# Turning the global heads' attention weights by DMA instead of on TensorE, in a window-attention and FFN kernel

## The chip, the cores and the metric

The kernel runs on one NeuronCore of one Trainium2 chip. The metric is the device time of one execution in microseconds (us); lower is better. Engine names are those of the profile: PE (TensorE matmul), PEld (TensorE weight load), DVE (VectorE), ACT (ScalarE), POOL (GpSimd), SP (SyncE, which here issues nearly all DMAs).

## The reference, cut to what matters

```python
# B, H, SL, SG, D = 8, 8, 512, 32, 64
k_all = np.concatenate([k_g, k_l], axis=2)           # 544 keys
s_g   = scale * np.matmul(q_g, k_all.transpose(0, 1, 3, 2))
out_g = np.matmul(sm(s_g), v_all)                    # 32 global queries see all 544 keys
s_ll  = np.where(np.abs(i - j) <= 32, scale * q_l @ k_l.T, -1e9)
a_l   = sm(np.concatenate([scale * q_l @ k_g.T, s_ll], axis=-1))
out_l = a_l @ np.concatenate([v_g, v_l], axis=2)     # 512 local queries, window of 32
x     = concat([out_g, out_l]) as [4608, 512]
h     = x @ w_in                                     # 512 -> 2048
g     = s * relu(h) ** 2 + b
out   = g @ w_out                                    # 2048 -> 512
```

In words: in each of 8 batches and 8 heads, 32 global queries attend to 544 keys and 512 local queries attend to their window and the 32 global keys. All 4608 rows then go through a feed-forward network (FFN) with a squared ReLU.

## The kernel before, in words

The program is one loop over 146 steps j. Step j computes the scores and the softmax of local head j (128 of them: batch, half of the sequence, head), and the FFN's first product for chunk m = j - 10 (`ffn_in`, 24 matmuls, L479) and its second product for chunk m - 1 (`ffn_out`, 12 matmuls, L512). There are 136 chunks of 2 x 128 hidden columns; 8 chunks make one tile of 256 rows. From step 18 on the order of PE, ACT and DVE is the order in which the code emits instructions. SP and POOL are placed by the scheduler.

One step, as it touches the change:

- PE: scores of head j (L352) with the global heads' product (L364) in between; every fourth step the product of weights and values of four local heads (`pv`, L319); `ffn_in` (L479); `ffn_out` of the chunk before (L512).
- DVE: masked scores with their minimum (L207), the sum into the global scores (L373), the sum and its reciprocal (L217, L218), the division (L223), four copies that part the f32 weights into two planes of 16-bit halves (L385, tile `two`), then for the FFN `r` (L486) and the low part of `g` (L494). `ffn_out` needs that low part with its third weight load.
- ACT: rounds keys and queries of the next head (L191, L193), one copy for the global scores (L372), the two exponentials (L214), joins the halves of the head before, once the DMA has turned them (L395, tile `turned`), then for the FFN the ReLU (L485) and the high part of `g` (L493).
- SP: loads, and one DMA transpose of `two` into `turned` per local head (L387).

So the local heads' weights are turned by DMA: part on DVE, turn by DMA, join on ACT one step later. Only the first 16 steps turn theirs on PE.

The global heads come in groups of four, `g` = 0 and 1 of each batch. Their scores are gathered in a tile `sg` of 128 rows (4 heads x 32 queries) by 544 keys. Their steps hang on s0 = 16 b + 12 for group 0 and 16 b + 16 for group 1: softmax (`g_softmax`) in step s0, the values' load in s0 + 2 (`g_load`), the turn in s0 + 3 (`g_transposes`), the product with the values in s0 + 5 (`g_pv`). The turn is five PE transposes of 128 x 128 (L419), four before `ffn_out`'s first half and one before its second, each followed by a copy from PSUM to the tile `pg` on ACT (L420). In ACT's order these copies stand behind the high part of `g` (L493), ahead of the next head's L191.

For batch 1, which the rows below show, group 0 has its softmax in step 28 and its turn in step 31, group 1 in steps 32 and 35. Step 35's `ffn_in` is chunk 25, and its `ffn_out` is chunk 24.

Of the kernel before, what the change touches and what calls it, by code (L numbers as in the profile page):

```python
# [10 lines left out]
F32 = mybir.dt.float32  # L11
# [4 lines left out]
I16 = mybir.dt.int16  # L16
# [5 lines left out]
P = 128  # L22
# [16 lines left out]
SGW = SL + SG  # L39
# [13 lines left out]
JOINED = [("pg", 1280), ("vsg", 1280)]  # L53
X_ACT = lambda i: i >= 4
G_AT = (12, 16)
G_TR = 3
G_LD = 2
G_PV = 5
GL_POOL = lambda m: False
# [8 lines left out]
def window_attention_then_ffn(ctx: ExitStack, tc: tile.TileContext, qd, qp, qg, kw, vw, vg, w_in, w_out, sv, bv, out):  # L68
    nc = tc.nc
# [3 lines left out]
    sb = ctx.enter_context(tc.tile_pool(name="sb", bufs=2))  # L73
    ps = ctx.enter_context(tc.tile_pool(name="ps", bufs=1, space=bass.MemoryType.PSUM))
# [3 lines left out]
    ident = const.tile([P, P], F32, name="ident")  # L78
# [18 lines left out]
    for first, parts in ((True, ((32, 192, 0),)), (False, ((0, 160, 0), (192, 224, 32)))):  # L97
# [3 lines left out]
        for c0, c1, skip in parts:  # L101
            for sign, base in ((1, c0 - skip), (-1, 64 - c0 + skip)):
                nc.gpsimd.affine_select(
                    out=mask[:, c0:c1], in_=mask[:, c0:c1], pattern=[[sign, c1 - c0]], compare_op=ALU.is_ge,
# [64 lines left out]
    st_ = {}  # L169
# [85 lines left out]
    def v_load(i):  # L255
        b, hf, h = slot(2 * i)
        rv = sb.tile([P, 2, 4 * D], F32, tag="rv", name=f"rvp{i}", bufs=2)
        nc.sync.dma_start(rv, vw[b, hf, h:h + 2].rearrange("h p f -> p h f"))
        st_["rvp", i] = rv
# [70 lines left out]
    def qg_load(b):  # L330
        rqg = sb.tile([P, 264], F32, tag="xr", name=f"rqg{b}", bufs=1)[:, 0:H * SG]
        nc.sync.dma_start(rqg, qg[b])
        st_["rqg", b] = rqg

    def qg_split(b):
        rqg = st_["rqg", b].rearrange("p (h q) -> p h q", h=H)
        qgs = sb.tile([P, H, 2, SG], F32R, tag="qgs", name=f"qgs{b}", bufs=1)
        nc.scalar.copy(out=qgs[:, :, 0, :], in_=rqg)
        nc.gpsimd.tensor_sub(out=qgs[:, :, 1, :], in0=rqg, in1=f32(qgs[:, :, 0, :]))
        st_["qgs", b] = qgs  # L340
# [34 lines left out]
    def late_scores(j):  # L375
        if ("late", j) in st_:
            p_g = ps.tile([P, 512], F32, tag="g", name=f"ps_g{j}")
            g_product(j, st_.pop(("late", j)), p_g)
            g_sum(j, p_g)
# [11 lines left out]
    def join(j):  # L391
        if j % 2 == 0:
            st_["ptp", j // 2] = sb.tile([P, 2, 4, P], F32, tag="pt", name=f"ptp{j // 2}")
        pt = st_["ptp", j // 2][:, j % 2]
        nc.scalar.copy(out=pt.bitcast(I16).rearrange("p c (q h) -> p c h q", h=2), in_=st_.pop(("turned", j)))  # L395
# [4 lines left out]
    def g_softmax(b, g):  # L400
        v = st_["sg", b, g]
        gm = sb.tile([P, 1], F32, tag="gm", name=f"gm{b}_{g}")
        gs = sb.tile([P, 1], F32, tag="gs", name=f"gs{b}_{g}")
        nc.vector.reduce_max(out=gm, in_=v, axis=mybir.AxisListType.X)
        nc.vector.tensor_scalar_mul(gm, gm, -scale)
        nc.scalar.activation(out=v, in_=v, func=AF.Exp, bias=gm, scale=scale, accum_out=gs)
        nc.vector.tensor_scalar_add(gs, gs, 1e-9)
        nc.vector.reciprocal(gs, gs)
        nc.vector.tensor_scalar_mul(v, v, gs)

    def g_transposes(b, g):
        sg = st_["sg", b, g]
        pg = sb.tile([P, 1280], F32, tag="pg", name=f"pg{b}_{g}", bufs=1)[:, 0:5 * P].rearrange("p (c r) -> p c r", c=5)
        st_["pg", b, g] = pg
        for c0, c1, tag in ((0, 4, "t"), (4, 5, "o")):
            p_t = ps.tile([P, 4, P], F32, tag=tag, name=f"ps_tg{b}_{g}_{c0}")
            for c in range(c0, c1):
                s0 = min(c * P, SGW - P)
                nc.tensor.transpose(out=p_t[:, c - c0, :], in_=sg[:, s0:s0 + P], identity=ident)  # L419
            nc.scalar.copy(out=pg[:, c0:c1], in_=p_t[:, 0:c1 - c0])  # L420
            yield

    def g_load(b, g):
        rv = st_["rvg", b, g] = sb.tile([P, 4, 5, D], F32, tag="vsg", name=f"rvg{b}_{g}", bufs=1)
        nc.sync.dma_start(rv.rearrange("p h c d -> p (h c d)"), vg[b, g])

    def g_pv(b, g):
        pg, rv = st_.pop(("pg", b, g)), st_.pop(("rvg", b, g))
        p_g = ps.tile([P, 512], F32, tag="t", name=f"ps_og{b}_{g}")
        for c in range(5):  # L430
            for n in range(4):
                m = slice(SG * n, SG * n + SG)
                nc.tensor.matmul(p_g[m, 0:D], lhsT=pg[:, c, m], rhs=rv[:, n, c], start=(c == 0), stop=(c == 4))  # L433
        og = sb.tile([P, P + 40], F32, tag="og", name=f"og{b}_{g}", bufs=1)[:, 0:D]
        nc.scalar.copy(out=og, in_=p_g[:, 0:D])
        rows = xg_d[b * SG:(b + 1) * SG, 4 * g * D:(4 * g + 4) * D]
        nc.sync.dma_start(rows.rearrange("q (h d) -> h q d", h=4), og)
# [60 lines left out]

    oacc = {}

    def ffn_out(m, turn):
        t, pr = m // 8, m % 8
        g = gs_.pop(m)
        if pr == 0:
            oacc[t] = [ps.tile([P, DM], F32, tag=f"acc{i}", name=f"acc{t}_{i}") for i in range(2)]
        for i in range(2):
            next(turn, None)
            n = 0
            for k in range(2):
                f = 2 * pr + k  # L510
                for a, e in ((0, 0), (0, 1), (1, 0)):
                    nc.tensor.matmul(  # L512
                        oacc[t][i], lhsT=g[:, a, k, i * P:(i + 1) * P], rhs=wo[f][:, e, :],
                        start=(pr == 0 and n == 0), stop=(pr == 7 and n == 5),
                    )
                    n += 1
        if pr == 7:
            for i in range(2):
                o = sb.tile([P, DM], F32, tag="r", name=f"o{t}_{i}", bufs=2)
                nc.scalar.copy(out=o, in_=oacc[t][i])  # L520
                if t < 16:
                    b, hf = t // 2, t % 2
                    r0 = b * (SL + SG) + SG + hf * HALF + i * P
                    nc.sync.dma_start(out[r0:r0 + P, :], o)
                else:
                    rows = out.rearrange("(b r) d -> b r d", r=SL + SG)[4 * i:4 * i + 4, 0:SG, :]
                    nc.sync.dma_start(rows, o)
# [3 lines left out]

    ENGINES = {getattr(mybir.EngineType, e) for e in ("PE", "Activation", "DVE")}
    NM = NT * 8
    early, gpv, turns = defaultdict(list), defaultdict(list), {}
    for b in range(B):
        for g in range(2):
            s0 = 16 * b + G_AT[g]
            early[s0].append(lambda b=b, g=g: g_softmax(b, g))
            turns[s0 + G_TR] = g_transposes(b, g)
            early[s0 + G_LD].append(lambda b=b, g=g: g_load(b, g))  # L540
            gpv[s0 + G_PV].append(lambda b=b, g=g: g_pv(b, g))

# [20 lines left out]
    for j in range(NM + LAG + 2):  # L563
        if j == ORDERED:
            fixed.enter_context(tc.manual_schedule(engines=ENGINES))
        sp(j + 1)
        if j + 4 < NF:
            ld(j + 4)
        if j + 2 >= NF:
            ld(j + 2)  # L570
        if NF <= j < NS and j % 4 == 2:
            for i in (j // 2 - 1, j // 2):
                v_load(i)
        for _ in range(CHUNKS_AT[j] if j < len(CHUNKS_AT) else 0):
            weight_chunk(chunk)
            chunk += 1
        if j < NS:
            b1 = j // 16 + 1
            if j % 16 == 14 and b1 < B:
                qg_load(b1)  # L580
            sc(j)
            if j % 16 == 15 and NF <= j + 1 < NS:
                qg_split(b1)
        tr(j - 1)
        pvs(j - 2)
        if NF <= j - 5 < NS and j % 4 == 1:
            pv((j - 5) // 2, 2)
        for fn in gpv.pop(j, []):
            fn()
        if NF <= j - 1 < NS:  # L590
            join(j - 1)
        if j == 0:
            vl32(0)
        vl32(j + 2)
        m = j - LAG
        for fn in early.pop(j, []):
            fn()
        if m == -1:
            x_split(0)
        then = []  # L600
        if 0 <= m < NM:
            t = m // 8 + 1
            if m % 8 == 7 and t < 16:
                then.append(lambda: x_split(t))
            ffn_in(m, then)
            late_scores(j)
            if m % 8 == 7 and t == 16:
                xg_split(16)
        else:
            for fn in then:  # L610
                fn()
        if 0 <= m - 1 < NM:
            ffn_out(m - 1, turns.pop(j, iter(())))
        else:
            list(turns.pop(j, ()))
    fixed.close()
    assert chunk == 16 and not gpv and not early

# [74 lines left out]
```

## Time and profile before

| | us |
|---|---|
| median of 3 runs (980.45 to 981.97) | 981.84 |
| the profiled execution | 982.35 |
| its span | 980.5 |
| PE busy | 948.3 (97%) |
| PE weight load busy | 846.3 (86%) |
| ACT busy | 714.6 (73%) |
| DVE busy | 651.0 (66%) |

The profiled execution lies 0.5 us above the median, and 1.9 us of it lie outside the span. Matmuls are pipelined and their ends are modelled, so a busy PE is not a PE at its peak. The rows below come from several views: groups of instructions by line, waits by pair, the chain of waits that ended last, and the timeline of single engines in order of time, merged where equal instructions follow each other.

### The profile page before, as it was taken

The page shows a single profiled execution, that of the slowest core. Times are in us where ns is not written, and L with a number is a line of the kernel's source. Part 1 is how long each engine was busy: PE and PEld are TensorE (multiplying, and loading weights), DVE is VectorE, ACT ScalarE, POOL GpSimd, SP SyncE. Part 2 cuts the span into 40 slices and gives each one's busy share as a digit, 9 for nine tenths or more (in the row PEclk, how much of TensorE's full clock was granted, in tenths as well). Part 3 has the DMA queues.
Part 4 walks back from the last instruction along what each step waited for, and adds up shares of the span by engine and source line. Part 5 has one row for each costly group of instructions (what it writes and reads, how often), then busy time and mean ns, then how long its engine had stood idle before and what let it go on. Part 6 is the DMA issues. An engine that isn't in the chain of part 4 may idle for free.

```text
span 980.5 us, 20198 instructions
## 1 busy us (share of the span) xinstructions
PE 948.3 (97%) x7380; PEld 846.3 (86%) x7380; DVE 651.0 (66%) x1996; ACT 714.6 (73%) x1510; POOL 217.4 (22%) x245
## 2 busy tenths in 40 slices
PE   6779999999999999999999999999999999999996
PEld 2457889999999999999999999999999999998995
DVE  5998766676767776677677766777667776742321
ACT  5986687777878787788788787788778787753221
POOL 1010322322323233232223232232323232300000
PEclk7669999999999999999999999999999999999999
DMA  8944335445544555535654464454543564220000
GB/s 308 341 163 147 99 98 129 106 109 137 133 99 114 130 135 111 108 98 133 132 116 99 129 153 90 117 124 109 135 115 90 143 133 101 71 62 35 11 12 22
DMA packets 177899, 115.09 MB, mean 117 GB/s; under 512 B 126088, under 2 KB 167048, under 8 KB 177800
## 3 DMA queue, kind: packets, MB, share of 16 engines
q1 hardware_dynamic: 177512, 112.76, 44.5%
q8 instruction: 58, 0.95, 0.4%
q10 hardware_dynamic: 288, 1.05, 0.3%
q14 instruction: 41, 0.34, 0.1%
HBM read 74.97 MB, written 9.44 MB: 86 GB/s over the span
## 4 chain that ended last, share of the span: by engine, by line
PE 91%; DVE 3%; DMA 3%; ACT 1%; SPq 0%; issue 0%; POOL 0%; POOLq 0%; ACTq 0%
PE ps_h L479 39%; PE acc L512 38%; PE ps_op L319 5%; PE ps_s L352 5%; PE ps_g L364 1%; PE ps_og L433 1%; DMA wst<-in_w_in 1%; PE ps_tg L419 1%; DMA b_t<-in_bv 1%; DVE we L161 1%; DMA wst<-in_w_out 1%; DVE wst L160 1%; DMA rkp<-in_kw 1%; DVE w L165 0%; DVE we L157 0%
## 5 line engine op out<-in xcount | busy, mean ns | idle before, releaser
L479 PE MATMUL ps_h<-xs,w 128*128 128x256 f32 x3264 | 412.7, 281 | 1.5 <-DVE nm L207 1.5
L512 PE MATMUL acc<-w,g 128*128 128x512 f32 x1632 | 403.6, 395 | 0.0
L479 PEld LDWEIGHTS ps_h<-xs,w 128*128 128x128 f32 x3264 | 395.0, 189 | 7.8 <-DVE nm L207 1.8
L512 PEld LDWEIGHTS acc<-w,g 128*128 128x128 f32 x1632 | 296.0, 188 | 58.4 <-DVE g L494 0.3
L192 POOL TENSOR_TENSOR kq<-rk,kq 64x416 fp32r<-64x416 f32 x112 | 125.4, 1120 | 628.5 <-ACT kq L191 600.5
L493 ACT ACTIVATE g<-r,b_t 128x512 fp32r<-128x512 f32 x136 | 98.5, 724 | 113.0 <-DVE r L486 113.0
L494 DVE SCALAR_TENSOR_TENSOR g<-r,b_t,g 128x512 fp32r<-128x512 f32 x136 | 103.0, 757 | 103.2 <-ACT g L493 103.2
L395 ACT COPY ptp<-turned 128x1024 int16<-128x1024 int16 x112 | 152.2, 1359 | 7.0 <-DMA turned<-two 7.0
L486 DVE SCALAR_TENSOR_TENSOR r<-ps_h,s_t,r 128x512 f32<-128x512 f32 x136 | 101.8, 748 | 68.6 <-ACT r L485 68.4
L485 ACT ACTIVATE r<-ps_h 128x512 f32<-128x512 f32 x136 | 81.4, 599 | 59.8 <-PE ps_h L479 54.0
L214 ACT ACTIVATE sm<-sm,nm 128x224 f32<-128x224 f32 (+1 forms) x256 | 117.8, 461 | 4.3 <-DVE nm L207 3.1
L385 DVE COPY two<-sm 128x256 int16<-128x256 int16 x448 | 100.1, 287 | 1.0 <-DMA turned<-two 1.0
L194 POOL TENSOR_TENSOR kq<-rq,kq 128x256 fp32r<-128x256 f32 x112 | 84.5, 755 | 8.8
L207 DVE CUSTOM_DVE_ANT_0 sm<-ps_s,mask 128x192 f32<-128x192 f32 (+1 forms) x224 | 74.3, 369 | 9.7 <-PE ps_s L352 9.7
L352 PE MATMUL ps_s<-kq 128*128 128x192 f32 (+1 forms) x448 | 78.0, 265 | 0.0
L352 PEld LDWEIGHTS ps_s<-kq 128*128 128x128 f32 x448 | 71.9, 189 | 6.9
L373 DVE TENSOR_TENSOR sg<-ps_g,tg 32x256 f32<-32x256 f32 (+1 forms) x112 | 48.3, 431 | 30.4 <-ACT tg L372 26.8
L223 DVE TENSOR_SCALAR sm<-sm,ss 128x192 f32<-128x192 f32 (+1 forms) x224 | 64.9, 332 | 3.9
L217 DVE TENSOR_SCALAR ss<-ss 128x2 f32<-128x2 f32 (+1 forms) x120 | 36.4, 303 | 45.6 <-ACT sm L214 45.1
L319 PE MATMUL ps_op<-ptp,rvp 128*64 128x128 f32 (+2 forms) x1024 | 61.4, 266 | 2.5 <-ACT ptp L310 2.3
L319 PEld LDWEIGHTS ps_op<-ptp,rvp 128*64 128x64 f32 x1024 | 52.7, 143 | 10.5 <-ACT ptp L310 4.2
L191 ACT CAST kq<-rk 64x416 fp32r<-64x416 f32 x112 | 59.8, 534 | 2.0 <-PE ps_s L352 0.7
(63 smaller groups left out, 644.7 us busy)
## 6 DMA issues: line engine op xcount, KB each, us to landing
rvp<-in_vw SPq DMA_DIRECT2D x64, 256.0 KB, 2.9
rq<-in_qd SPq DMA_DIRECT2D x112, 128.0 KB, 2.3
rk<-in_kw SPq DMA_DIRECT2D x56, 208.0 KB, 2.5
rvg<-in_vg SPq DMA_DIRECT2D x16, 640.0 KB, 5.7
out<-o SPq DMA_DIRECT2D x34, 256.0 KB, 2.0
wst<-in_w_in SPq DMA_DIRECT2D x15, 512.0 KB, 4.0
wst<-in_w_out SPq DMA_DIRECT2D x15, 512.0 KB, 6.9
turned<-two SPq DMA_TRANSPOSE x112, 3.1
```

The costliest lines, as they stand in the source:

```text
L192: (nc.gpsimd if K_POOL(j) else nc.vector).tensor_sub(out=ks[p1:p1 + 64], in0=rk[p0:p0 + 64], in1=f32(ks[p0:p0 + 64]))
L194: nc.gpsimd.tensor_sub(out=qs[:, 1, :], in0=rq, in1=f32(qs[:, 0, :]))
L214: nc.scalar.activation(out=p, in_=p, func=AF.Exp, bias=nm[:, n:n + 1], scale=-1.0, accum_out=ss[:, n:n + 1],)
L319: nc.tensor.matmul(p_o[64 * k:64 * k + 64, u, blk, q0:q0 + w], lhsT=rv[:, k, v:v + D], rhs=pt[:, k, o] if i < NF // 2 else pt[:, k, 2 * bl ...
L352: nc.tensor.matmul(p_s[:, cols], lhsT=qs[:, a, blk * P:(blk + 1) * P], rhs=ks[:, cols], start=(a == 0), stop=(a == 1),)
L385: nc.vector.tensor_copy(out=two[:, 2 * blk + c], in_=sm[:, :, c0:c0 + P])
L395: nc.scalar.copy(out=pt.bitcast(I16).rearrange("p c (q h) -> p c h q", h=2), in_=st_.pop(("turned", j)))
L479: nc.tensor.matmul(p_h[:, k], lhsT=wi[f][:, a, c, :], rhs=xs[:, e, c, :], start=(n == 0), stop=(n == 11),)
L486: nc.vector.scalar_tensor_tensor(out=r, in0=p_h, scalar=s_t, in1=r, op0=ALU.mult, op1=ALU.mult)
L493: nc.scalar.activation(out=g[:, 0], in_=r, func=AF.Identity, bias=b_t)
L494: nc.vector.scalar_tensor_tensor(out=g[:, 1], in0=r, scalar=b_t, in1=f32(g[:, 0]), op0=ALU.add, op1=ALU.subtract,)
L512: nc.tensor.matmul(oacc[t][i], lhsT=g[:, a, k, i * P:(i + 1) * P], rhs=wo[f][:, e, :], start=(pr == 0 and n == 0), stop=(pr == 7 and n == 5),)
```

## The change

The five PE transposes and the two ACT copies of a group go. In step s0 + 2 DVE parts `sg` into two planes of 16-bit halves (five copies into a new tile `gtwo`) and SP issues one DMA transpose of its ten blocks of 128 x 128. In step s0 + 3 ACT joins the halves into f32 with one copy of 1280 16-bit elements a row. Both results lie in the two halves of the buffer `pg`, which keeps its size.

```diff
-G_TR = 3
+G_TR = 2
...
-    def g_transposes(b, g):
-        sg = st_["sg", b, g]
-        pg = sb.tile([P, 1280], F32, tag="pg", ...)[:, 0:5 * P].rearrange("p (c r) -> p c r", c=5)
-        for c0, c1, tag in ((0, 4, "t"), (4, 5, "o")):
-            p_t = ps.tile([P, 4, P], F32, tag=tag, ...)
-            for c in range(c0, c1):
-                s0 = min(c * P, SGW - P)
-                nc.tensor.transpose(out=p_t[:, c - c0, :], in_=sg[:, s0:s0 + P], identity=ident)
-            nc.scalar.copy(out=pg[:, c0:c1], in_=p_t[:, 0:c1 - c0])
-            yield
+    def g_turn(b, g):
+        sg = st_["sg", b, g].bitcast(I16).rearrange("p (k h) -> p h k", h=2)
+        both = sb.tile([P, 4 * 5 * P], I16, tag="pg", ...)
+        turned, pg = both[:, 0:10 * P], both[:, 10 * P:20 * P]
+        two = sb.tile([P, 5, 2, P], I16, tag="gtwo", ..., bufs=1)
+        for c in range(5):
+            s0 = min(c * P, SGW - P)
+            nc.vector.tensor_copy(out=two[:, c], in_=sg[:, :, s0:s0 + P])
+        turned = turned.rearrange("p (c h q) -> p c h q", c=5, h=2)
+        nc.sync.dma_start_transpose(turned..., two...)
+
+    def g_join(b, g):
+        turned, pg = st_.pop(("turned_g", b, g))
+        nc.scalar.copy(out=pg.rearrange("p (c q h) -> p c h q", c=5, h=2), in_=turned)
...
-            turns[s0 + G_TR] = g_transposes(b, g)
+            early[s0 + G_TR].append(lambda b=b, g=g: g_turn(b, g))
+            early[s0 + G_TR + 1].append(lambda b=b, g=g: g_join(b, g))
```

DVE, step 34 (batch 1, group 1; a name's number is the step or chunk). Before:

```order
L223 TENSOR_SCALAR sm34_2781<-sm34_2781,ss34_2780 128x224
L385 COPY two34_2793<-sm34_2781 128x256 x4
L486 SCALAR_TENSOR_TENSOR r24_2828<-ps_h24_2803,s_t_71,r24_2828 128x512
L494 SCALAR_TENSOR_TENSOR g24_2831<-r24_2828,b_t_72,g24_2831 128x512
L207 ISA sm35_2868,nm35_2866<-ps_s35_2859,mask1_104 128x192
```

DVE, step 34, in the changed kernel:

```order
L223 TENSOR_SCALAR sm34_2778<-sm34_2778,ss34_2777 128x224
L385 COPY two34_2790<-sm34_2778 128x256 x4
L418 COPY gtwo1_1_2799<-sg20_1466 128x256 x5
L493 SCALAR_TENSOR_TENSOR r24_2833<-ps_h24_2808,s_t_71,r24_2833 128x512
L501 SCALAR_TENSOR_TENSOR g24_2836<-r24_2833,b_t_72,g24_2836 128x512
L207 ISA sm35_2873,nm35_2871<-ps_s35_2864,mask1_104 128x192
```

The five copies stand between the local head's copies and the FFN's `r`.

ACT, step 35 and the start of step 36. Before:

```order
L395 COPY ptp17_2887<-turned34_2798 128x4x2x128
L485 ACTIVATE r25_2914<-ps_h25_2889 128x512
L493 ACTIVATE g25_2917<-r25_2914,b_t_72 128x512
L420 COPY pg1_1_2922<-ps_tg1_1_0_2923 128x512
L420 COPY pg1_1_2922<-ps_tg1_1_4_2935 128x128
L191 CAST kq37_2944<-rk36_2764 64x416
```

ACT at the same place in the changed kernel:

```order
L395 COPY ptp17_2892<-turned34_2795 128x4x2x128
L427 COPY pg1_1_2798<-pg1_1_2798 128x5x2x128
L492 ACTIVATE r25_2920<-ps_h25_2895 128x512
L500 ACTIVATE g25_2923<-r25_2920,b_t_72 128x512
L191 CAST kq37_2940<-rk36_2761 64x416
```

The work on `pg` moves from behind `g` of the FFN to ahead of its ReLU, and is one copy in place of two.

## Rows read from the trace of the kernel before

**Rows 1.** The page: busy time by engine, then the chain's shares by line.

```profile
PE 948.3 (97%) x7380; PEld 846.3 (86%) x7380; DVE 651.0 (66%) x1996; ACT 714.6 (73%) x1510; POOL 217.4 (22%) x245
...
PE ps_h L479 39%; PE acc L512 38%; PE ps_op L319 5%; PE ps_s L352 5%; PE ps_g L364 1%; PE ps_og L433 1%; DMA wst<-in_w_in 1%; PE ps_tg L419 1%; DMA b_t<-in_bv 1%; DVE we L161 1%; DMA wst<-in_w_out 1%; DVE wst L160 1%; DMA rkp<-in_kw 1%; DVE w L165 0%; DVE we L157 0%
```

**Rows 2.** The chain of waits, 205 to 260 us: start, us, what.

```profile
240.24 2.83 PE ps_h L479 x24
243.07 0.44 PE ps_tg L419 x4
243.51 1.39 PE acc L512 x6
244.90 0.11 PE ps_tg L419
```

**Rows 3.** Waits, 170 to 870 us: total, times, longest.

```profile
DVE sm L207 <- PE ps_s L352: 4.2, 13, 0.4
...
PEld ps_op L319 <- issue: 0.4, 1, 0.4
```

**Rows 4.** Groups by line: busy, mean ns of one | idle before.

```profile
L395 ACT COPY ptp<-turned 128x1024 int16<-128x1024 int16 x112 | 152.2, 1359 | 7.0 <-DMA turned<-two 7.0
...
L385 DVE COPY two<-sm 128x256 int16<-128x256 int16 x448 | 100.1, 287 | 1.0 <-DMA turned<-two 1.0
```

**Rows 5.** Timeline of DVE, steps 30 and 34 to 36: start, us, instruction.

```profile
210.79 0.89 DVE L385 COPY two<-sm 128x256 int16<-128x256 int16 x4
211.69 0.75 DVE L486 SCALAR_TENSOR_TENSOR r<-ps_h,s_t,r 128x512 f32<-128x512 f32 x1
...
238.68 0.89 DVE L385 COPY two<-sm 128x256 int16<-128x256 int16 x4
239.55 0.75 DVE L486 SCALAR_TENSOR_TENSOR r<-ps_h,s_t,r 128x512 f32<-128x512 f32 x1
...
246.54 0.74 DVE L486 SCALAR_TENSOR_TENSOR r<-ps_h,s_t,r 128x512 f32<-128x512 f32 x1
248.08 0.75 DVE L494 SCALAR_TENSOR_TENSOR g<-r,b_t,g 128x512 fp32r<-128x512 f32 x1 [0.79 <-ACT g L493]
...
254.43 0.75 DVE L494 SCALAR_TENSOR_TENSOR g<-r,b_t,g 128x512 fp32r<-128x512 f32 x1 [0.79 <-ACT g L493]
```

**Rows 6.** Timeline of ACT, steps 31 and 35, to the next step's first cast.

```profile
215.54 1.37 ACT L395 COPY ptp<-turned 128x1024 int16<-128x1024 int16 x1
216.94 0.60 ACT L485 ACTIVATE r<-ps_h 128x512 f32<-128x512 f32 x1
...
218.98 0.73 ACT L420 COPY pg<-ps_tg 128x512 f32<-128x512 f32 x2
219.74 0.54 ACT L191 CAST kq<-rk 64x416 fp32r<-64x416 f32 x1
...
244.47 1.34 ACT L395 COPY ptp<-turned 128x1024 int16<-128x1024 int16 x1
245.84 0.60 ACT L485 ACTIVATE r<-ps_h 128x512 f32<-128x512 f32 x1
```

**Rows 7.** PEld: `ffn_out`'s loads 2 and 3 (chunk 25), load 3 (chunk 26).

```profile
249.62 0.42 PEld L512 LDWEIGHTS acc<-w,g 128*128 128x128 f32 x2
...
258.44 0.19 PEld L512 LDWEIGHTS acc<-w,g 128*128 128x128 f32 x1
```

**Rows 8.** The same place in batch 6: the low part on DVE, the third load.

```profile
785.89 0.75 DVE L494 SCALAR_TENSOR_TENSOR g<-r,b_t,g 128x512 fp32r<-128x512 f32 x1 [0.79 <-ACT g L493]
...
787.54 0.19 PEld L512 LDWEIGHTS acc<-w,g 128*128 128x128 f32 x1
```

**Rows 9.** The turned tile: issue on SP (ns min/median/max) and landing.

```profile
L387 SPq DMA_TRANSPOSE turned<-two x104: 1231/1233/2402, 169.7 to 862.5; - x104
...
DMA to landing us min/median/max: 3.0/3.1/5.0
```

**Rows 10.** Timeline of SP, steps 30 and 34.

```profile
211.76 1.23 SPq L387 DMA_TRANSPOSE turned<-two  x1
...
239.64 1.24 SPq L387 DMA_TRANSPOSE turned<-two  x1
```

**Rows 11.** Timeline of PE in the start: a wait.

```profile
78.09 0.93 PE L319 MATMUL ps_op<-ptp,rvp 128*64 128x128 f32 x14 [2.11 <-ACT ptp L310]
```

**Rows 12.** Two stretches: busy PE, PEld, DVE, ACT, POOL; then PEclk.

```profile
75.79:79.20 3.41, 1.30 (x16) 1.05 (x16) 3.41 (x11) 1.76 (x3) 0.00 (x0) 1.00 0.73 286
79.20:82.62 3.42, 3.42 (x9) 2.18 (x8) 1.72 (x3) 3.42 (x10) 0.00 (x0) 0.50 0.74 246
```

More of the change, by code (lines that the diff above doesn't have):

```diff
@@ L409, in g_softmax @@
         nc.vector.tensor_scalar_mul(v, v, gs)
-    def g_transposes(b, g):
-        sg = st_["sg", b, g]
-        pg = sb.tile([P, 1280], F32, tag="pg", name=f"pg{b}_{g}", bufs=1)[:, 0:5 * P].rearrange("p (c r) -> p c r", c=5)
-        st_["pg", b, g] = pg
-        for c0, c1, tag in ((0, 4, "t"), (4, 5, "o")):
-            p_t = ps.tile([P, 4, P], F32, tag=tag, name=f"ps_tg{b}_{g}_{c0}")
-            for c in range(c0, c1):
-                s0 = min(c * P, SGW - P)
-                nc.tensor.transpose(out=p_t[:, c - c0, :], in_=sg[:, s0:s0 + P], identity=ident)
-            nc.scalar.copy(out=pg[:, c0:c1], in_=p_t[:, 0:c1 - c0])
-            yield
+    def g_turn(b, g):
+        sg = st_["sg", b, g].bitcast(I16).rearrange("p (k h) -> p h k", h=2)
+        both = sb.tile([P, 4 * 5 * P], I16, tag="pg", name=f"pg{b}_{g}", bufs=1)
+        turned, pg = both[:, 0:10 * P], both[:, 10 * P:20 * P]
+        two = sb.tile([P, 5, 2, P], I16, tag="gtwo", name=f"gtwo{b}_{g}", bufs=1)
+        for c in range(5):
+            s0 = min(c * P, SGW - P)
+            nc.vector.tensor_copy(out=two[:, c], in_=sg[:, :, s0:s0 + P])
+        turned = turned.rearrange("p (c h q) -> p c h q", c=5, h=2)
+        nc.sync.dma_start_transpose(
+            turned.rearrange("p c h q -> p (c h) q"), two.rearrange("p c h k -> p (c h k)"),
+        )
+        st_["turned_g", b, g] = turned, pg
+    def g_join(b, g):
+        turned, pg = st_.pop(("turned_g", b, g))
+        nc.scalar.copy(out=pg.rearrange("p (c q h) -> p c h q", c=5, h=2), in_=turned)
+        st_["pg", b, g] = pg.bitcast(F32).rearrange("p (c r) -> p c r", c=5)
     def g_load(b, g):
@@ L499, in window_attention_then_ffn, with ffn_out @@
     oacc = {}
-    def ffn_out(m, turn):
+    def ffn_out(m):
         t, pr = m // 8, m % 8
@@ L506, in ffn_out @@
         for i in range(2):
-            next(turn, None)
             n = 0
@@ L533, in window_attention_then_ffn @@
     NM = NT * 8
-    early, gpv, turns = defaultdict(list), defaultdict(list), {}
+    early, gpv = defaultdict(list), defaultdict(list)
     for b in range(B):
@@ L612, in window_attention_then_ffn @@
         if 0 <= m - 1 < NM:
-            ffn_out(m - 1, turns.pop(j, iter(())))
-        else:
-            list(turns.pop(j, ()))
+            ffn_out(m - 1)
     fixed.close()
```

## The prediction

> **What bounds the kernel now.** I read the page first: PE is busy for 97% of the span, and nine tenths of the chain that ended last lie on PE's two FFN products [rows 1]. By that alone, whatever leaves PE shortens the run. The second view is the chain of waits in a steady stretch. It shows what the five transposes are worth there: 0.44 + 0.11 = 0.55 us for a group, with PE's neighbours following at once [rows 2]. The third view is the waits between 170 and 870 us: PE and its weight loads waited once, 0.4 us in all, so PE sets the pace. But the other side is nearly as slow: in 700 us DVE waited only 13 times for scores from PE, 4.2 us together [rows 3]. DVE and ACT wait for each other instead. So I read their timelines through batch 1. From step 25 to step 36 they pass the work to and fro (exponentials, division, copies, ReLU, `r`, `g`, low part) with no wait for PE at all. What they lose in that stretch is carried from step to step, and only the distance between them and PE hides it.
>
> That distance is what the forecast rests on. It is smallest where `ffn_out` of chunk 25 wants `g`'s low part, two steps after the second global softmax. The low part is done at 248.08 + 0.75 = 248.83 [rows 5]. PE's third weight load, which reads it, starts at 249.62 + 0.42 - 0.19 = 249.85 [rows 7]: 1.02 us of cover. In batch 6 the same place has 787.54 - 786.64 = 0.90 us [rows 8]. The batches 1 to 6 all have this place, and read in the same way the four between them have 0.63 to 0.96. I take 0.9 for each of the six. A step later PE also does the products with the values, and the cover is 258.44 - 255.18 = 3.3 us [rows 5, 7].
>
> **The change part by part.**
>
> *PE.* Five transposes go from each of 16 groups: 16 x 0.55 = 8.8 us if nothing else changes [rows 2].
>
> *DVE, step s0 + 2.* Five copies of the same form as the local head's four. Those run in 0.89 us, the last lasting 0.287 [rows 4, 5], so one follows another after (0.89 - 0.287)/3 = 0.20 us. Behind them on DVE stands the FFN's `r`; ACT waits for `r`, and the next head's masked scores stand behind the low part. In step 34 `r` could start after nine copies at 238.68 + 1.80 = 240.48 in place of 239.55: +0.93. In step 30: 210.79 + 1.80 = 212.59 in place of 211.69: +0.90 [rows 5]. No row has these copies with the global tile as source; were each to cost its full 0.287, it would be 1.44, and less than 0.9 I see no reason for.
>
> *ACT, step s0 + 3.* The join of a local head takes 1024 elements a row, and what follows starts 1.37 to 1.40 us after it [rows 6]; 1280 elements are 1.25 times as many: 1.71 us. It stands ahead of the ReLU, for which `r`, ACT's own `g` and the low part wait in turn. The bounds are 1.36 us, as if length didn't count [rows 4], and 1.71. I take 1.71.
>
> *ACT, behind `g`.* The two copies from PSUM go: the next cast came 219.74 - 218.98 = 0.76 us after their start [rows 6]. That is given back, but only after the low part of that step.
>
> *The DMA.* The turn of ten blocks is issued on SP behind the local head's of eight. Eight blocks keep SP for 1.23 us and land 3.1 us after the issue [rows 9]. I take 1.25 times as much, 3.9, as an estimate. In step 30 SP is free of the local turn at 211.76 + 1.23 = 212.99 [rows 10], so it lands at 216.9. ACT gets to the join at 215.54 + 1.37 + 0.90 = 217.8: 0.9 us to spare. In step 34 more than 3 us are to spare. So I cost the DMA at nothing, with DVE's lateness as its cover. What SP issues behind it, loads for two to four steps on, has the same cover as before.
>
> *The sum.* At the low part of chunk 25, DVE and ACT are late by 0.90 + 1.71 - 0.76 (group 0), plus 0.93 + 1.71 (group 1) = 4.49. In step 35 the ReLU ended at 246.44 and `r` started at 246.54 [rows 5, 6], so up to 0.1 of it was already waited: 4.4. Less the cover of 0.9, PE stands 3.5 us later in each batch, in pieces, the first at chunk 21's `ffn_out` in step 32. What PE saved on transposes is swallowed here: it comes to the same load sooner and waits longer. After step 36 the lateness of DVE and ACT (3.7) and of PE (3.5) are nearly equal, the cover is 3.3 us, and the next batch starts as before. So the six batches add up: 6 x 3.5 = 21 us. Batch 0 has its groups in and just behind the start, where the weights are converted; batch 7 has its second group where no local heads are left. For these two I take nothing, with -2 (all transposes saved) and +4 as ends.
>
> 982.35 + 21 = 1003.4 for the profiled execution; the median lies 0.5 below its own, so 1003.
>
> With a join of 1.36 the lateness is 0.7 less, 6 x 2.8 = 17: 999, or 997 with the two outer batches. With copies of 0.287 it is about 1.0 more, 6 x 4.5 = 27: 1009, or 1013 with them. This forecast's own range is 997 to 1013.
>
> The Trainium skill speaks against the change too: VectorE: DVE Perf Modes, section "The three transpose paths", puts a 128 x 128 turn at 390 ns on TensorE and 1309 ns by DMA, and its "Rules for kernel authors" say to use TensorE where the result may land in PSUM. The trace has about 0.11 us of PE's time for one block [rows 2] and 3.1 us for eight by DMA [rows 9]. By the rule's prices the DMA alone would cost 10 x 1.3 = 13 us a group (an estimate); by the trace it is hidden, and the cost lies in the copies around it.
>
> **Rivals.**
>
> *A. PE's saving comes through.* For it: PE's 97% [rows 1], and `g`'s cover is over 2 us in most steps. Then 982.35 - 8.8 - 0.5 = 973. Against it: at chunk 25 the cover is 0.9 and the copies and joins sum to 4.4. It decides the sign: it needs a lateness under about 0.9 there. The Trainium skill, in Perfetto Trace Analysis, section "Identifying the Most-Contended Engine", says to improve the engine with the highest occupancy first, with weight-load busy as TensorE's measure; by that rule, too, the time would be this rival's. Chance 0.07.
>
> *B. The batch's groups don't add up.* The long step 33, with both products, lets DVE and ACT catch up, so that group 1 starts anew. Then a batch costs 0.93 + 1.71 - 0.1 - 0.9 = 1.6 for group 1 and up to 0.7 for group 0: 10 to 14 us, 992 to 996. Against it: nothing on DVE or ACT waited for PE in this stretch, so a longer PE step is already counted in the cover. Chance 0.13.
>
> *C. The DMA comes late.* If the second turn waits for the first, or takes the 5.0 us of the slowest local turn [rows 9] times 1.25, it lands at 212.99 + 6.25 = 219.2, and ACT waits 1.4 us more in group 0: 6 x 1.4 = 8.4 on top, 1012. Chance 0.10.
>
> *D. The clock falls.* In the start PE waited 2.11 us [rows 11], and in the stretch after that the granted clock was 0.50, the level of 1.2 GHz [rows 12]. The forecast's 3.5 us a batch come in several pieces, each shorter than that wait. If two stalls a batch each brought such a stretch of 3.4 us at half clock, that is 1.7 us each: 6 x 2 x 1.7 = 20 on top, 1023. Chance 0.05.
>
> **How the numbers follow.** The forecast has 0.61; A 0.07, B 0.13, C 0.10, D 0.05; 0.04 is left for a standstill, where losses and the saving cancel within 0.2% (about 2 us, what a measurement of this kernel can tell from no change). So faster 0.07, same 0.04, slower 0.89. The range takes in the forecast's own and B's and C's times, 992 to 1013, and leaves out A, D and the standstill (0.16).
>
> **What would show it.** Right: PE waits for DVE's low part of `g` (third weight load of `ffn_out`) and for POOL's keys in steps 31 to 36 of each batch, near 3.5 us a batch, and none in the rest; the join on ACT near 1.7 us; `r` late by about 0.9 in steps s0 + 2; no wait of ACT for the global turn. The first term to doubt is the join's length, the second the claim that nothing catches up between group 0 and group 1. Wrong: PE without waits and 8.8 us shorter (A), waits in group 1 only (B), ACT waiting for the turned tile (C), or clock below 1.00 after a stall (D).

## The result and the profile after

The changed kernel takes 995.75 us, the median of 4 runs (995.22 to 996.51), beside 981.90 us for the kernel before on the same chip (980.45 to 982.54): 1.0144 times as long, with a 95% interval of 1.0126 to 1.0161. Its profiled execution took 995.83 us, its span is 994.0 us. That is 13.5 us more than the span of before.

The page of the changed kernel, busy time by engine and then the chain's shares by engine, stands against [rows 1]:

```profile
PE 950.2 (96%) x7300; PEld 837.9 (84%) x7300; DVE 668.3 (67%) x2076; ACT 727.7 (73%) x1494; POOL 216.1 (22%) x245
...
PE 48%; ACT 25%; DVE 18%; issue 4%; DMA 3%; SPq 1%; ACTq 0%
```

The chain's shares by engine in the kernel before:

```profile
PE 91%; DVE 3%; DMA 3%; ACT 1%; SPq 0%; issue 0%; POOL 0%; POOLq 0%; ACTq 0%
```

80 transposes have left PE, and its busy time has not fallen: it was 948.3 and is 950.2 us. The weight loads fell by 8.4 us. The chain tells more: nine tenths of it lay on PE, and now PE has 48%, ACT 25% and DVE 18%. Nearly half of the chain is now work that passes between ACT and DVE, and PE waits for it.

The waits of the changed kernel between 170 and 880 us (who waits, for whom: total, times, longest) stand against [rows 3], where PE's loads waited once, 0.4 us:

```profile
PEld acc L518 <- ACT g L500: 7.9, 7, 1.3
PEld acc L518 <- DVE g L501: 7.5, 18, 0.5
PE acc L518 <- ACT g L500: 6.5, 7, 1.1
...
PEld acc L518 <- ACT o L526: 3.8, 6, 0.7
PEld ps_h L486 <- ACT xs L456: 3.4, 6, 0.6
DVE sm L207 <- PE ps_s L352: 3.2, 9, 0.4
PEld ps_s L352 <- POOL kq L194: 2.9, 6, 0.6
...
PEld ps_s L352 <- POOL kq L192: 0.3, 1, 0.3
```

The loads wait 7.9 + 7.5 + 3.8 + 3.4 + 2.9 + 0.3 = 25.8 us. They all lie in the batches 1 to 6, 4.2 to 4.7 us in each. (The waits of PE itself are the same ones seen from the product behind the load, so they are not added.)

To see where the time went I took the start of the first `ffn_in` product of a chunk on PE's timeline, in both traces, and subtracted. Here are chunk 13, ahead of batch 1's global heads, and chunk 135, the last of all: first of the kernel before (start, us, instruction), then of the changed one.

```profile
160.03 3.00 PE L479 MATMUL ps_h<-xs,w 128*128 128x256 f32 x24
...
963.18 2.96 PE L479 MATMUL ps_h<-xs,w 128*128 128x256 f32 x24
```

```profile
154.85 3.00 PE L486 MATMUL ps_h<-xs,w 128*128 128x256 f32 x24
...
976.70 2.96 PE L486 MATMUL ps_h<-xs,w 128*128 128x256 f32 x24
```

PE is 5.2 us ahead at chunk 13 (and still at chunk 15) and 13.5 us behind at the end. Worked out in the same way, changed minus before:

| chunk | 3 | 9 | 15 | 31 | 47 | 63 | 79 | 95 | 111 | 125 | 135 |
|---|---|---|---|---|---|---|---|---|---|---|---|
| us | -4.7 | -4.6 | -5.2 | -2.1 | 1.0 | 4.2 | 7.3 | 10.7 | 13.9 | 13.5 | 13.5 |

So there are three parts. The start gains 5.2 us between these two executions. Each batch from 1 to 6 then loses 3.1 to 3.5 us, 19.1 together. Batch 7 gives back 0.4. The 25.8 us of waits fit this: 19.1 us of it is seen as PE's lateness, and the other 6.7 is about what the 12 groups saved on transposes, 12 x 0.55 = 6.6 us. PE came to its load earlier by what it had saved, and waited that much longer.

Batch 1, step by step, in the changed kernel. DVE's timeline of the second group (start, us, instruction, idle before it) answers to [rows 5]:

```profile
236.07 1.09 DVE L418 COPY gtwo<-sg 128x256 int16<-128x256 int16 x5
237.08 0.74 DVE L493 SCALAR_TENSOR_TENSOR r<-ps_h,s_t,r 128x512 f32<-128x512 f32 x1
...
245.51 0.75 DVE L493 SCALAR_TENSOR_TENSOR r<-ps_h,s_t,r 128x512 f32<-128x512 f32 x1 [1.37 <-ACT r L492]
247.05 0.75 DVE L501 SCALAR_TENSOR_TENSOR g<-r,b_t,g 128x512 fp32r<-128x512 f32 x1 [0.79 <-ACT g L500]
```

ACT's timeline, the join of group 0 and that of group 1, answers to [rows 6]:

```profile
212.50 1.65 ACT L427 COPY pg<-pg 128x1280 int16<-128x1280 int16 x1
214.17 0.60 ACT L492 ACTIVATE r<-ps_h 128x512 f32<-128x512 f32 x1
...
241.99 1.33 ACT L395 COPY ptp<-turned 128x1024 int16<-128x1024 int16 x1
243.20 1.66 ACT L427 COPY pg<-pg 128x1280 int16<-128x1280 int16 x1
244.88 0.60 ACT L492 ACTIVATE r<-ps_h 128x512 f32<-128x512 f32 x1
```

And the loads of `ffn_out` of chunk 25 answer to [rows 7]:

```profile
247.07 0.30 PEld L518 LDWEIGHTS acc<-w,g 128*128 128x128 f32 x2 [1.27 <-ACT g L500]
247.86 2.15 PEld L518 LDWEIGHTS acc<-w,g 128*128 128x128 f32 x10 [0.49 <-DVE g L501]
```

The low part of chunk 25 starts at 247.05, before it was 248.08. Measured against the 5.18 us by which the whole stretch lies earlier, it is late by 5.18 - 1.03 = 4.15 us. The same subtraction at the chunks before gives 0.9 at chunk 20, 2.4 at 21, 1.75 at 22 and 23 (the two copies from PSUM are given back), 2.7 at 24 and 4.15 at 25. Of that the cover took 1.02 us, and 4.15 - 1.02 = 3.13 us is left for PE; the table has 3.1. The low part ends at 247.80, and the load that reads it starts at 247.86: the cover that was 1.02 us is used up.

The turn itself on SP (issue in ns min/median/max, first and last start), and who waited for its tile, answer to [rows 9]:

```profile
L420 SPq DMA_TRANSPOSE pg<-gtwo x16: 1335/1405/1616, 99.1 to 894.3; - x16
...
  ACT pg L427: 1.4, 1
```

Once in 16 groups ACT waited for the turned tile, 1.4 us, and that was in the start.

What the start gained is seen on ACT, and not in the global heads' work. ACT in the kernel before, around the wait of [rows 11]:

```profile
76.42 1.22 ACT L156 ACTIVATE wst<-wst,mid_b 128x1024 int32<-128x1024 uint32 x1 [2.57 <-DMA wst<-in_w_out]
77.54 0.49 ACT L310 COPY ptp<-ps_t 128x416 f32<-128x416 f32 x1
```

And the same two instructions in the changed kernel:

```profile
72.11 0.51 ACT L310 COPY ptp<-ps_t 128x416 f32<-128x416 f32 x1
...
75.63 1.24 ACT L156 ACTIVATE wst<-wst,mid_b 128x1024 int32<-128x1024 uint32 x1 [1.90 <-DMA wst<-in_w_out]
```

L310 copies weights that PE has turned in the start, and PE waits for it. The scheduler, which orders the start, put it behind L156 before; L156 waits for a load, and L310 waited with it. In the changed kernel it stands ahead. PE's wait of 2.11 us at 78.09 is gone, and the two stretches of [rows 12] read (busy PE, PEld, DVE, ACT, POOL; then the granted clock):

```profile
75.79:79.20 3.41, 3.41 (x18) 2.52 (x18) 3.41 (x12) 2.28 (x3) 0.00 (x0) 1.00 0.67 242
79.20:82.62 3.42, 3.42 (x28) 3.24 (x27) 2.64 (x5) 3.42 (x11) 0.00 (x0) 1.00 0.69 202
```

In the first stretch PE is busy for 3.41 us and not for 1.30. In the second the granted clock is 1.00, the level of 2.4 GHz; after the wait it had been 0.50.

### The profile page after: what moved, and what is told of

Read it like the earlier page. It is cut to its first block, busy times and chain, and to the rows that moved or that the text cites. A ratio compares the mean times of both kernels' runs of the same rounds, so it can differ in the third digit from the quotient of the medians.

```text
span 994.0 us, 20133 instructions
## 1 busy us (share of the span) xinstructions
PE 950.2 (96%) x7300; PEld 837.9 (84%) x7300; DVE 668.3 (67%) x2076; ACT 727.7 (73%) x1494; POOL 216.1 (22%) x245
## 4 chain that ended last, share of the span: by engine, by line
PE 48%; ACT 25%; DVE 18%; issue 4%; DMA 3%; SPq 1%; ACTq 0%
PE ps_h L486 21%; PE acc L518 20%; ACT sm L214 6%; DVE r L493 4%; ACT g L500 3%; ACT ptp L395 3%; PE ps_op L319 3%; ACT kq L191 3%; DVE two L385 3%; ACT tg L372 2%; PE ps_s L352 2%; ACT pg L427 2%; ACT kq L193 2%; DVE gtwo L418 1%; DVE g L501 1%
## 5 line engine op out<-in xcount | busy, mean ns | idle before, releaser
L192 POOL TENSOR_TENSOR kq<-rk,kq 64x416 fp32r<-64x416 f32 x112 | 124.6, 1112 | 643.7 <-ACT kq L191 621.9
L194 POOL TENSOR_TENSOR kq<-rq,kq 128x256 fp32r<-128x256 f32 x112 | 84.0, 750 | 8.8
```

Of the source, the lines that this page charges most:

```text
L192: (nc.gpsimd if K_POOL(j) else nc.vector).tensor_sub(out=ks[p1:p1 + 64], in0=rk[p0:p0 + 64], in1=f32(ks[p0:p0 + 64]))
```

## The experiments

Every kernel below but the third is the changed kernel with the edit shown; the third is the kernel before with its edit. `g_transposes` and the table `turns` are those of the kernel before: the transposes by PE and the two copies from PSUM, inside `ffn_out`. "Shift" is the difference of PE's arrival, kernel minus before, at a chunk, as in the table above. The first four share their runs of before (median 981.23), and so do the next four (981.03) and the last two (980.51).

**Only batch 0 by DMA.** The scheduler gives the start the same order of L310 and L156 as in the changed kernel; the steady batches are those of before.

```
+            if b == 0:
                 early[s0 + G_TR].append(lambda b=b, g=g: g_turn(b, g))
                 early[s0 + G_TR + 1].append(lambda b=b, g=g: g_join(b, g))
+            else:
+                turns[s0 + 3] = g_transposes(b, g)
```

> Only batch 0's two groups are turned by DMA; the other 14 groups keep the PE transposes. Theory (the start): the changed kernel reached chunk 15 of the FFN 5.2 us earlier than before, since ACT's order in the start came out differently (the copy of turned weights L310 ahead of a weight conversion that waits for its DMA); this kernel has that same order, so it should gain those 5.2 us and nothing else: 976.7. Rival (only the work counts): 982 less two groups of 0.55 = 980.8.

Measured: 977.76 us, ratio 0.9962 (0.9950 to 0.9975). The shift is -4.3 at chunk 15 and stays there to the end. With batch 0's part of the change alone the time falls by 3.5 us by the medians, and nothing in the rest takes that away; the rival's 980.8 lies outside the interval. How much of it the order makes is said at the next kernel.

**Batches 1 to 7 by DMA, batch 0 by PE.** The same edit with `b > 0`.

> Batches 1 to 7 are turned by DMA, batch 0 by PE; ACT's order in the start is that of before. Theory: no gain in the start, 6 x 3.15 us lost in batches 1 to 6 and 0.4 gained in batch 7: 982 + 18.9 - 0.4 = 1000.5. Rival (the start's gain is not tied to batch 0's change): 995.

Measured: 999.87 us, ratio 1.0185 (1.0170 to 1.0201). The shift goes from -0.5 at chunk 31 to 15.3 at chunk 111 and is 14.8 at the end; batch 1 starts at -3.5. So the six batches cost 18.8 us, as in the changed kernel, and batch 7 gives 0.4 back. (The profiled execution took 997.62 us, 2.2 less than the median.) One thing did not go as I thought: here L310 stands behind L156 again, at 75.55 us, but PE waits 1.57 us for it, and the stretch after it has no half clock. The wait's length differs between kernels with the old order (2.11, 1.57, and 1.37 and 1.17 in the next two), and the half clock after it is in the trace of before alone. So the 5.2 us is the gap between two profiled executions, and not the worth of the order. In all kernels of this section the new order comes with batch 0 by DMA, and the old one with batch 0 by PE. By the traces the three with the old order reach chunk 15 ahead of the profiled execution of before by 3.5, 2.8 and 2.1 us, though their start is that of before, and those with the new order by 4.3 to 5.7. The order is therefore worth 0.8 to 3.6 us in the traces; the rest lies with that one execution of before, with its longer wait and its half clock. By the medians the two kernels give -3.5 and +18.6 us, 15.2 together, and the change gave 13.9.

**No turn in batches 1 to 7.** Neither copies nor DMA nor transposes; the product with the values reads the identity in place of the turned weights, so that PE does that product as before.

```
-            turns[s0 + G_TR] = g_transposes(b, g)
+            if b == 0:
+                turns[s0 + G_TR] = g_transposes(b, g)
...
-                nc.tensor.matmul(p_g[m, 0:D], lhsT=pg[:, c, m], ...)
+                nc.tensor.matmul(p_g[m, 0:D], lhsT=ident[:, m] if pg is None else pg[:, c, m], ...)
```

> The kernel before with the turn of the global weights left out in batches 1 to 7: no transposes, no copies from PSUM, and the product with the values reads the identity in their place. Theory: with nothing added on DVE and ACT, PE's 14 x 0.55 us come through: 982 - 7.7 = 974.3. Rival (DVE and ACT set the pace all through the steady part): they lose only 0.76 us a group on ACT, and PE's saving is waited away: 980 to 982.

Measured: 972.31 us, ratio 0.9908 (0.9893 to 0.9923). The shift is -2.8 at chunk 15 and -10.7 at chunk 125: 7.9 us for 14 groups, 0.57 each, where [rows 2] gave 0.55. PE's saving is real, and it comes through to the end when nothing is added on DVE and ACT. Rival A fails by what was added, not because PE's work was hidden.

**Group 0 by DMA, group 1 by PE, in batches 1 to 7.** The edit of the first kernel with `b > 0 and g == 0`. It tells the carried lateness from rival B: if group 1 starts anew, group 0 alone, whose lateness is 0.90 + 1.71 - 0.76 before the cover, must cost next to nothing by the end of a batch.

> In batches 1 to 7 group 0 is turned by DMA and group 1 by PE. Theory (lateness is carried to chunk 25, cover 0.9 us): DVE and ACT are late there by 0.93 + 1.65 - 0.76 = 1.8, so PE loses 0.9 a batch: 982 + 6 x 0.9 = 987.5. Rival (the batch's long step lets them catch up, so only the stall of chunk 21 counts, less the saved transposes): 0 to 0.2 a batch, 982 to 983.

Measured: 985.90 us, ratio 1.0050 (1.0037 to 1.0063). The shift is -1.3 at chunk 31 and 2.95 at chunk 111, 0.85 us a batch over five batches. Group 0's share is still there when the batch ends. The low parts show it directly. Measured as in batch 1 above, they are late by 1.6 to 1.8 us at chunk 22 and its like in the batches 1 to 6, and three chunks later still by 1.6 to 1.8. Nothing is caught up there. The cost of group 0 alone is not far from B's bound of 0.7, but with both groups a batch costs 3.2, so group 1 adds 2.3 where B had 1.6.

**The parting copies on POOL.** This takes one term, 0.9 us twice a batch, off DVE.

```
-            nc.vector.tensor_copy(out=two[:, c], in_=sg[:, :, s0:s0 + P])
+            nc.gpsimd.tensor_copy(out=two[:, c], in_=sg[:, :, s0:s0 + P])
```

> The changed kernel with the five parting copies of each group on POOL in place of DVE. Theory (terms add up to the lateness at chunk 25): 2 x 0.93 go, 1.65 - 0.76 + 1.65 = 2.5 stay, less the cover of 0.9: 1.6 a batch, 6 x 1.6 = 10 in place of 19, with the start's 4.8 kept: 986. Rival (POOL is late with the next head's keys, whose cover is about 1 us): the gain is lost again, 990 or more.

Measured: 986.04 us, ratio 1.0052 (1.0038 to 1.0065). The shift grows by 1.8 us a batch (-5.7 at chunk 15, 4.9 at chunk 111), where the change has 3.2. The copies take 400 ns each on POOL (median), and PE's loads wait for POOL's keys 1.5 us in all between 170 and 880 us, against 2.9 + 0.3 in the changed kernel.

**The join on POOL.** The other term, 1.7 us twice a batch.

```
-        nc.scalar.copy(out=pg.rearrange("p (c q h) -> p c h q", c=5, h=2), in_=turned)
+        nc.gpsimd.tensor_copy(out=pg.rearrange("p (c q h) -> p c h q", c=5, h=2), in_=turned)
```

> The changed kernel with the join of each group on POOL in place of ACT. Theory: 0.93 - 0.76 + 0.93 = 1.1 stay, 0.2 above the cover: 6 x 0.2 = 1 in place of 19: 977.5. Rival (POOL late with the keys: one join keeps it some 3 to 4 us, its gaps are 4 to 5): 1 to 3 us a group, 990.

Measured: 1008.14 us, ratio 1.0277 (1.0262 to 1.0291). My theory was wrong here: ACT was relieved, and the kernel got 12 us slower than the changed one. POOL's timeline shows why:

```profile
241.36 1.65 POOL L427 COPY pg<-pg 128x1280 int16<-128x1280 int16 x1 [6.59 <-DMA pg<-gtwo]
243.08 1.06 POOL L192 TENSOR_TENSOR kq<-rk,kq 64x416 fp32r<-64x416 f32 x1
244.22 0.89 POOL L194 TENSOR_TENSOR kq<-rq,kq 128x256 fp32r<-128x256 f32 x1
```

And its waits between 170 and 880 us:

```profile
POOL pg L427 <- DMA pg<-gtwo: 42.4, 7, 7.5
PEld ps_s L352 <- POOL kq L192: 14.6, 6, 2.9
...
PEld ps_g L364 <- POOL qgs L339: 6.5, 6, 2.0
```

The copy itself is no longer than on ACT. But POOL stands for 6.6 us before it, until the turned tile has landed, and the next keys (L192, L194) and PE's scores are queued behind. The rival was right that POOL is late with the keys, but not why: it had the join at 3 to 4 us, and the join takes 1.65; the wait for the tile comes on top. The shift grows by 5.4 us a batch, and the rival's 990 was too low.

**Both on POOL.** The two edits together.

> The changed kernel with both the parting copies and the join on POOL, so DVE gets nothing and ACT loses 0.76 us a group. Theory: PE's saving comes through in full, 16 x 0.55 = 8.8, beside about 4 in the start: 969. Rival (POOL late with the keys): 980 or more.

Measured: 975.24 us, ratio 0.9945 (0.9933 to 0.9958): the lowest median of the kernels that compute everything, and 2% below the changed one. Against before it is ahead by half a percent, and its interval overlaps with those of the first kernel and of the next but one, so which of the three is fastest is not shown. With the copies on POOL the turn starts two steps sooner: in batch 1's second group the copies start at 221.69 us, against 236.32 on DVE in the kernel with the join alone on POOL. The join still waits for its tile (4.52 us in the row below), but PE's loads now wait only 1.9 us in all for POOL's L192 and L194. The shift is -4.5 at chunk 15, -4.4 at chunk 111, -5.6 at the end: the batches cost nothing now, but they don't give the 1.1 us each of the third kernel either. Between 170 and 880 us PE's loads wait 5.7 us for the low part (10 times) beside the 1.9 for the keys. Of the 5.7, 3.3 come where the join runs. POOL in the second group of batch 1:

```profile
230.27 1.66 POOL L427 COPY pg<-pg 128x1280 int16<-128x1280 int16 x1 [4.52 <-DMA pg<-gtwo]
```

DVE beside it, and the load that waits for DVE:

```profile
230.56 1.86 DVE L501 SCALAR_TENSOR_TENSOR g<-r,b_t,g 128x512 fp32r<-128x512 f32 x1 [0.79 <-ACT g L500]
```

```profile
232.47 2.15 PEld L518 LDWEIGHTS acc<-w,g 128*128 128x128 f32 x10 [0.56 <-DVE g L501]
```

The low part, 0.75 us everywhere in the steady part of before, takes 1.86 us when POOL's join runs at the same time, and PE's load waits for its end. Such a low part stands in the batches 1, 3, 5 and 6.

**The join behind `g` on ACT.** The join is issued after `ffn_in` of its step, so ReLU and `g` go ahead of it.

```
-            early[s0 + G_TR + 1].append(lambda b=b, g=g: g_join(b, g))
+            late[s0 + G_TR + 1].append(lambda b=b, g=g: g_join(b, g))
```

> The changed kernel with the join behind the FFN's g on ACT (where the copies from PSUM stood before) in place of ahead of the ReLU. Theory: the low part of chunk 25 is late by 0.93 + 0.89 + 0.93 = 2.75 only, but the keys of the next head are late by 0.89 more, 3.64 against their own cover of 0.5 to 0.9: 2.9 a batch, so hardly a gain: 994. Rival (only the FFN's low part counts): 1.85 a batch, 987.5.

Measured: 992.33 us, ratio 1.0115 (1.0102 to 1.0129). The shift grows by 2.6 us a batch in place of 3.2. In its waits between 170 and 880 us the scores now wait for POOL's keys more often than in the changed kernel:

```profile
PEld ps_s L352 <- POOL kq L194: 6.2, 12, 0.6
...
PEld ps_s L352 <- POOL kq L192: 2.6, 7, 0.4
```

ACT's casts for the keys now stand behind the join, and the keys have little cover of their own. This move changes who waits, and gains 0.5 us a batch.

**One group each, the join late.** In batches 1 to 6 group 0 goes by PE and group 1 by DMA, with copies on POOL (that line is left out below) and the join and the product with the values two steps later; batches 0 and 7 as changed.

```
+            late = 2 if g == 1 and 0 < b < B - 1 else 0
+            if b in (0, B - 1) or g == 1:
                 early[s0 + G_TR].append(lambda b=b, g=g: g_turn(b, g))
+                early[s0 + G_TR + 1 + late].append(lambda b=b, g=g: g_join(b, g))
+            else:
+                turns[s0 + 3] = g_transposes(b, g)
...
+            gpv[s0 + G_PV + late].append(lambda b=b, g=g: g_pv(b, g))
```

> Batches 0 and 7 as in the changed kernel. In batches 1 to 6 group 0 is turned by PE as before; group 1 is turned by DMA with its parting copies on POOL, its join on ACT two steps later (step 37 in place of 35 for batch 1, where the cover is 3.3 us) and its product with the values two steps later too. Theory: nothing is added ahead of chunk 25, so the five transposes saved come through, 0.55 a batch: 981.1 - 4.5 (start) - 3.3 - 0.4 = 973. Rival (DVE is held up by POOL's copies, as the low part of 1.86 us beside POOL's copy in the kernel with both on POOL): 0.5 to 1 us a batch, 976 to 979.

Measured: 976.83 us, ratio 0.9958 (0.9945 to 0.9970): the rival's time, but its mechanism only in part. The shift is -4.7 at chunk 15 and -5.4 at chunk 111, 0.1 us gained a batch where 0.55 was hoped for. The waits between 170 and 880 us have these two lines:

```profile
ACT ptp L395 <- DMA turned<-two: 6.4, 8, 1.5
...
PEld acc L531 <- DVE g L513: 2.5, 7, 0.5
```

Batches 1 and 2 gain 0.46 and 0.44 us, and none of PE's loads waits in them. In the batches 3 to 6 loads wait 2.6 us, 2.0 of it for the low part. POOL's copies lengthen one low part of each batch from 0.75 to 0.92 or 0.93 us, which is a small part of that. In batches 3, 4 and 6 ACT waits 0.66, 0.76 and 0.83 us for a local head's turned tile a few steps earlier, and from there DVE and ACT are late by 0.8 to 0.9 us more. The kernel before has such waits too (6.5 us, 8 times), at other places; what moves them is open.

**The same with `late = 0`.**

> As the mixed kernel, but group 1's join and product with the values at their old places (join in step 35 for batch 1, ahead of chunk 25's ReLU). Theory: the join alone, 1.65, less the cover of 0.9: 0.75 lost a batch: 981.1 - 4.5 + 4.5 - 0.4 = 980.7. Rival (the place of the join doesn't matter, as ACT is busy for 73% only): 973.

Measured: 982.84 us, ratio 1.0021 (1.0011 to 1.0030); the shift grows by 0.8 us a batch, where I had put 0.75. Where the join and the product stand is worth 6 us: ahead of the ReLU of chunk 25's step the join finds little cover, two steps later it finds enough. The distance that the prediction started from is what decides.

## Why the prediction was right, and where it was not

The forecast was 982.35 + 21 = 1003.35 us for the profiled execution, and that took 995.83, 7.5 less. The sign and the way to it came out as said: of the 7.5 us the six batches account for 1.9 and the outer batches for 5.6. The forecast's own range, 997 to 1013, misses the result. The range as stated, 992 to 1013, holds it because rival B's times were taken in, and B did not occur; that part was luck.

*What bounds the kernel.* Right. PE's 97% hid a second line of work, DVE and ACT, only 0.6 to 1.0 us ahead of PE's need at the closest places of each batch. One reading was off: the "nine tenths" of the chain lie on PE as a whole, and the two FFN products have 39 + 38 = 77% [rows 1]. The third kernel shows that PE's saving counts, the chain of the changed kernel that the added work counts for more. The Trainium skill's rule in Perfetto Trace Analysis, section "Identifying the Most-Contended Engine", would improve the busiest engine first. The third kernel agrees with it: with the turn left out, which takes work off PE and a little off ACT, PE arrives 7.9 us sooner. In the changed kernel, where DVE and ACT got work in exchange, the time rose by 13.9 us.

*The closest place.* The prediction has it at chunk 25 and its like in the other batches. Read in the same way, the low part two chunks earlier has less cover in five of the six batches, 0.75 to 0.88 us, and in batch 1 it is 0.88 at chunk 23. The sum does not suffer, since the lateness there is only 1.75. But the 0.85 us of the fourth kernel is decided there: in batch 1 PE has lost its 0.8 us by the start of chunk 25.

*The copies on DVE.* Predicted 0.90 and 0.93; the low part of chunk 20 was late by 0.9. Five copies last 1.09 us, but the `r` behind them starts 237.08 - 236.07 = 1.01 us after the first, by DVE's rows above.

*The join.* Predicted 1.71; it takes 1.65 (median). On the path it is a little less: in [rows 6] the ReLU started 1.37 us after the local join, and with the global join between them 244.88 - 241.99 = 2.89, so 1.52 us more. Two joins, 0.2 less each, are why the lateness is 4.15 and not 4.4.

*The copies from PSUM.* Predicted -0.76; between chunks 21 and 22 the lateness fell by 2.4 - 1.75 = 0.65.

*The DMA at nothing.* Right: one wait of 1.4 us in the start. Where POOL stands waiting for the tile, in two of the experiments, it has it 3.5 and 3.6 us after the issue, where the prediction took 3.9. Rival C did not occur.

*The cover and the sum.* Predicted 3.5 a batch and 21 for six; measured 3.2 and 19.1. Where the swallowed saving should show, it does (25.8 us of waits against 19.1 of lateness). The waits that I named, for the low part and for POOL's keys, make only 7.5 + 2.9 + 0.3 = 10.7 us of the 25.8. PE also waits for the high part of `g` on ACT (7.9, the largest), for ACT's split of `xs` (3.4) and for its output copies (3.8): all stand behind the same joins on ACT.

*The outer batches.* This is the term that failed: "For these two I take nothing, with -2 ... and +4 as ends". The profiles have -5.2 and -0.4, and by the medians of the first kernel batch 0 alone gives -3.5. The end of -2 priced the transposes and forgot the order. I had [rows 11, 12] before me, a wait of 2.11 us and a stretch at half clock after it, and used them for rival D alone; that ACT's copy stood there behind an instruction that waits for a load, and that any change of the scheduler's input could bring it ahead, would have taken the lower end to about -4. Part of the 5.2 is also that the profiled execution of before was slow in its start. With the measured terms 982.35 + 19.1 - 5.2 - 0.4 = 995.85, and the profiled execution took 995.83; that is bookkeeping and no test, as the three terms are differences of the same two traces.

*Rivals.* A came out the wrong way, as the time rose. B's time, 992 to 996, holds the result, and B is still wrong. It says that a batch costs 1.6 for group 1 and up to 0.7 for group 0 because DVE and ACT catch up between them. The lateness was 1.75 at chunk 23, with nothing caught up, and the fourth kernel's group 0 costs 0.85 us a batch to the end. The forecast and B's upper end lie 7 us apart, and the start's term that neither of them had is 5.2: the time alone could not tell them apart. D did not occur: the granted clock is 1.00 in the steady part, though PE's loads waited 25.8 us there in pieces of up to 1.3 us. The page has it in 40 slices of the span (9 is 90% or more):

```profile
PEclk8669999999999999999999999999999999999999
```

## What to carry to other kernels

Before taking work off the busiest engine, look for the engine that comes next at the place where the two are closest, and compare the work added there with that distance: 4.15 us against 1.02 decided this change, not the 8.8 us that PE saved. An instruction that waits for a transfer holds up everything queued behind it, so a helper's engine is chosen by what stands behind it and not by its idle share: POOL, idle for three quarters of the span, made the slowest kernel of all with the join alone, and one 2% faster than the changed kernel with the copies and the join. And where a scheduler orders a part of the program, any edit may reorder a part that it doesn't touch; that term belongs in the range.

## What the runs showed of the hardware

POOL's copies hold DVE's low part up. The low part (two inputs from SBUF) takes 0.75 us in the steady part of before and of the changed kernel. Beside the last of POOL's five parting copies it takes 0.92 to 0.93, and beside POOL's join of 1.66 us it takes 1.86 in the rows above, and 1.98, 1.85, 1.90 and 1.52 at other places of that kernel. In these five it ends 0.48 to 0.49 us after the join does, whenever it began.

The kernel before shows that the order counts. POOL's L192, which reads two tiles in SBUF, runs beside a low part 82 times. In 81 it starts behind the low part's start, and the low part keeps its 0.75 us. Once it starts 0.39 us ahead, and the low part takes twice as long:

```profile
111.71 1.41 POOL L192 TENSOR_TENSOR kq<-rk,kq 64x416 fp32r<-64x416 f32 x1
```

```profile
112.10 1.57 DVE L494 SCALAR_TENSOR_TENSOR g<-r,b_t,g 128x512 fp32r<-128x512 f32 x1
```

The Trainium skill has the rule, in SBUF — State Buffer, section "Who interferes with whom": a DVE instruction with two inputs in SBUF contends with a GpSimd instruction that reads SBUF, the shared port pair is an exclusive lock, and the order of issue decides who is blocked. By that the low part beside the join would end 0.75 us after the copy's end, at 230.27 + 1.66 + 0.75 = 232.68 (an estimate); the trace has 230.56 + 1.86 = 232.42, 0.3 us sooner. That the first one holds the other up agrees. No run here changed the low part's inputs, so that the shared ports are the cause was not tried.

The strided 16-bit copy of 1280 elements a row takes about the same on both engines: 1.65 us on ACT, and 1.65 and 1.69 on POOL in the two kernels with the join there (medians). I had expected 3 to 4 us on POOL.
